# A quarter of the tokens per partition group for two small computations, and a plan that knows GpSimd's port, in a fused attention kernel

## The chip, the cores and the metric

One core of a Trainium2 chip. The metric is the device time of one execution in microseconds, the median of several. A comparison is a ratio: the mean time of one kernel's fast runs over the mean of the other's fast runs of the same rounds, with a 95% interval, so it is not quite the ratio of the medians quoted beside it. In the profile PE is the matrix engine TensorE, PEld its weight loads, ACT is ScalarE, DVE is VectorE, POOL is GpSimd and SP the engine that issues the transfers. PSUM is the memory, in banks, that PE's results go to.

## The reference

Two attentions over the same 2048 tokens (640 features, 32 heads of 20), mixed by a gate. A is full attention, B looks at eight earlier tokens two apart.

```python
g = sigmoid((x * gate_w).sum(-1, keepdims=True))
a = A_ref(x, A_wqkv, A_wo)      # softmax(q k^T * scale) v over all 2048 keys, 32 heads
b = B_ref(x, B_wqkv, B_wo)      # softmax over 8 taps: keys at s, s-2, ..., s-14, masked below 0
return g * a + (1 - g) * b
```

## The kernel before

The kernel is written as generators of tasks. A small scheduler in the same file puts the tasks in order **before** the program exists: it keeps a clock for each engine, with a planned duration for each task and a latency for each engine's results, and decides with it which task comes next on each engine. The chip then runs that fixed order. An engine whose next instruction isn't ready waits, whatever else is ready.

```python
LAT = {"pe": 0.18, "act": 0.06, "dve": 0.08, "pool": 0.1, "sp": 0.1}   # planned latency of results, us
PLAN = {                     # settings of the planner, from the n-th tile of exponentials on
    0: ((0.3, 0.7), 0.26, 2.5, 1.0, 1.0, -1.0, 0.0, 12.0, 7.0, 9.64, ...),
    # ... 56 rows more (cut)
}
# in task(): when may it start, by the plan's clock?
start = self.avail[stream]
for d in t.deps:
    start = max(start, d.end + LAT[d.stream])
```

A's scores are computed by PE in units of 512 keys by queries, 2048 units in all. Two or three units make a tile that ScalarE exponentiates (`ebuf`). Some units, called rides, are left to VectorE: an integer approximation (`uD`) in four shifted copies (`eD`), for which GpSimd scales the values (`vS`). Each such unit costs PE four value products in place of one.

```python
# A: upper bounds of the scores, from |q| and the keys' maxima; 32 partitions, 512 tokens
ins = e.matmul(side[b][0:32, :], KMd[:, ff, :], qabs[qq][:, :], start=(k == 0), stop=(k == len(fl) - 1), ...)
T("dve", dvc(512), lambda e, b=b: e.tensor_scalar(qbnd[0:32, :], side[b][0:32, :], 1.0, STEP * TOP, ...), ...)
# B: gate and denominators; 128 partitions, of which groups of 32 hold the same heads, 256 tokens
mms = [(side[b][:, TOK:2 * TOK], gwrep(c), xT[:, c, t0:t0 + TOK]) for c in range(CN)]
mms = [(side[b][:, 0:TOK], Rep[:, :], eB[:, hh * TOK:(hh + 1) * TOK]) for hh in range(2)]
T("act", actc(TOK), lambda e, b=b: e.activation(tB[:, :], side[b][:, TOK:2 * TOK], ACTF.Tanh, scale=0.5), ...)
t = TB(TOK * 7.5e-3, lambda e, b=b: e.reciprocal(rB[:, :], side[b][:, 0:TOK]), ...)
release(b, t)                # the bank of PSUM may be used again after the reciprocal
# A: the shifted copies of a ride, and the scaled values for them
T("dve", 0.11 + 0.1334 * n, lambda e, k=k, sl=sl: e.tensor_scalar(eD[:, sl % NS, ...], uD[...], SHIFTS[k], ...), ...)
T("pool", 1.0, lambda e: e.tensor_tensor(vS[:, d % 2, :, :], ..., ALU.mult), ...)
```

## Time and profile before

| | before |
|---|---|
| time, median | 850.85 us |
| ScalarE, first to last exponential | 815.8 us |
| of it, its work back to back | 777.8 us |
| of it, lost | 38.0 us |
| PE fillers (sets of four matmuls, run where the plan has nothing else for PE) | 306 |
| rides on VectorE | 328 of 2048 units |

"Work back to back" counts each activation at the distance to its successor when none waits (904 ns for 1024 columns, 1331 ns for 1536, 477 ns for 512, 264 ns for 256, read from the start times); "lost" is the rest. (The prediction put the two at 816.3 and 38.5 us; here the last exponential ends at its start plus its distance.) These rows of the groups by form, besides those that the prediction shows, are needed later. After the bar come busy time in us and the mean of one in ns, after the second bar the engine's idle time before it.

```profile
L792 DVE TENSOR_SCALAR eD<-uD 128x2048 int16<-128x2048 int16 x246 | 174.1, 734 | 3.0 <-PE obank L1545 2.3
L784 POOL TENSOR_TENSOR vS<-vA,vw 128x252 bf16<-128x252 bf16 x82 | 62.9, 769 | 259.7 <-PE obank L1545 259.7
L864 DVE TENSOR_TENSOR stage<-qkvB 128x1280 bf16<-128x1280 bf16 x64 | 53.7, 866 | 0.1
```

The waits (who for whom, us in total, times, longest):

```profile
PEld score L1477 <- ACT ebuf L1500: 105.9, 268, 1.3
PE score L1477 <- ACT ebuf L1500: 6.8, 17, 1.0
PEld score L1477 <- DVE uD L1490: 24.2, 55, 1.1
```

The reader should see that PE's matmuls hardly wait for ScalarE (6.8 us), and not conclude that PE is short of time. Its weight loads wait 105.9 us for ScalarE, mostly while PE is busy with something else (all its idle time is 848.7 - 821.5 = 27.2 us), and 306 fillers of 0.216 us are another 66 us in which the plan had nothing for it.

### The profile page before, as it was taken

The numbers are of one execution on the slowest core, as the hardware profiler recorded it, in microseconds if no ns is written. First come the engines' busy times: TensorE is split into PE (matmuls) and PEld (weight loads), VectorE is DVE, ScalarE is ACT, GpSimd is POOL, SyncE is SP. The second block draws the span as 40 slices with busy tenths as digits, with TensorE's granted clock in tenths as the row PEclk, the third lists the DMA queues.
The fourth block names the chain that finished last, engine by engine and source line by source line (L and its number), as shares of the span: only waits on it lengthen the run. The fifth ranks groups of instructions, "written<-read, shape, count | busy, mean of one in ns | idle before, by whom it ended". The sixth has DMA issues, their size and how long they took to land.

```text
span 848.7 us, 30119 instructions
## 1 busy us (share of the span) xinstructions
PE 821.5 (97%) x12957; PEld 299.7 (35%) x12957; DVE 716.4 (84%) x1212; ACT 809.6 (95%) x770; POOL 142.0 (17%) x181
## 2 busy tenths in 40 slices
PE   8999999999999999999999999999999999999997
PEld 4432232334333343334334243333332333333233
DVE  7566887889899797989888898989998897999973
ACT  4999999999999999999999999999999999999994
POOL 5031014501122110111100111111011111012110
PEclk9999999999999999999999999999999999999999
DMA  9011212001010010011001011010010001001000
GB/s 314 23 40 42 48 31 73 15 13 33 26 27 22 25 42 20 21 25 27 16 16 37 6 20 44 20 31 11 19 32 20 7 20 41 15 7 40 17 6 33
DMA packets 40889, 28.13 MB, mean 33 GB/s; under 512 B 23732, under 2 KB 39556, under 8 KB 40756
## 3 DMA queue, kind: packets, MB, share of 16 engines
q1 hardware_dynamic: 40756, 26.20, 11.8%
q8 instruction: 103, 1.69, 0.8%
q14 instruction: 30, 0.25, 0.1%
HBM read 11.94 MB, written 2.62 MB: 17 GB/s over the span
## 4 chain that ended last, share of the span: by engine, by line
PE 73%; ACT 14%; DVE 8%; issue 5%; SPq 0%; DMA 0%; DVEq 0%; ACTq 0%
PE score L1477 22%; PE obank L1545 18%; PE side L554 16%; ACT ebuf L1500 13%; PE score L554 8%; PE obank L1566 4%; DVE eD L792 2%; PE score L1566 2%; DVE uD L1490 1%; PE side L878 1%; DVE stage L864 1%; PE score L1193 1%; PE obank L457 1%; DVE oN L767 1%; PE score L680 0%
## 5 line engine op out<-in xcount | busy, mean ns | idle before, releaser
L1500 ACT ACTIVATE ebuf<-score 128x1024 bf16<-128x1024 f32 (+1 forms) x738 | 796.5, 1187 | 17.6 <-PE score L1477 14.7
L1477 PE MATMUL score<-qT,kT 32*128 32x512 bf16 x2048 | 295.0, 384 | 9.9 <-ACT ebuf L1500 6.8
L1490 DVE TENSOR_SCALAR uD<-score 128x512 int16<-128x512 f32 x328 | 220.9, 684 | 45.7 <-PE score L1477 42.0
L792 DVE TENSOR_SCALAR eD<-uD 128x2048 int16<-128x2048 int16 x246 | 174.1, 734 | 3.0 <-PE obank L1545 2.3
L1477 PEld LDWEIGHTS score<-qT,kT 32*128 32x128 bf16 x2048 | 72.9, 91 | 263.9 <-ACT ebuf L1500 105.9
L1545 PE MATMUL obank<-ebuf,vA 128*21 128x512 bf16 x1720 | 160.1, 385 | 4.6 <-DVE eD L792 3.5
L784 POOL TENSOR_TENSOR vS<-vA,vw 128x252 bf16<-128x252 bf16 x82 | 62.9, 769 | 259.7 <-PE obank L1545 259.7
L554 PE MATMUL side<-xT,kvw 128*32 128x256 bf16 (+1 forms) x2470 | 101.7, 281 | 0.7 <-DVE qkvB L848 0.6
L1545 PE MATMUL obank<-eD,vS 128*21 128x512 bf16 x984 | 86.0, 379 | 0.0
L760 POOL TENSOR_TENSOR rcp<-rcp,gA 128x16 f32<-128x16 f32 x31 | 12.3, 395 | 386.6 <-DVE rcp L758 367.2
L554 PEld LDWEIGHTS side<-xT,kvw 128*32 128x32 bf16 x2470 | 58.4, 96 | 34.9 <-issue 16.7
L1545 PEld LDWEIGHTS obank<-ebuf,vA 128*21 128x21 bf16 x1720 | 38.6, 89 | 89.3 <-issue 72.9
L1566 PE MATMUL obank<-xT,zero 128*32 128x512 bf16 x688 | 58.5, 383 | 0.0
L864 DVE TENSOR_TENSOR stage<-qkvB 128x1280 bf16<-128x1280 bf16 x64 | 53.7, 866 | 0.1
L941 DVE TENSOR_TENSOR stage<-qkvB,repB 128x1280 bf16<-128x1280 bf16 x64 | 52.6, 848 | 1.0 <-DMA repB<-eB 1.0
L554 PE MATMUL side<-stage,ident 128*32 128x512 bf16 (+1 forms) x736 | 46.7, 345 | 1.0 <-DVE oB L956 0.5
L848 DVE CAST qkvB<-side 128x512 bf16<-128x512 f32 (+1 forms) x70 | 40.5, 587 | 6.4 <-PE side L554 6.4
L765 POOL TENSOR_TENSOR oN<-oTt,rcp 128x512 bf16<-128x512 f32 x31 | 34.8, 1123 | 2.4
L1566 PE MATMUL score<-xT,ident 128*32 128x512 bf16 x380 | 33.7, 381 | 0.0
L1545 PE MATMUL obank<-uD,vA 128*21 128x512 bf16 x328 | 31.9, 379 | 0.0
L754 DVE STREAM_TRANSPOSE oTt<-obank 128x512 f32<-128x512 f32 x32 | 22.8, 712 | 8.9 <-PE obank L1545 8.6
L1545 PEld LDWEIGHTS obank<-eD,vS 128*21 128x21 bf16 x984 | 24.5, 91 | 15.5 <-issue 1.8
(175 smaller groups left out, 622.8 us busy)
## 6 DMA issues: line engine op xcount, KB each, us to landing
repB<-eB SPq DMA_DIRECT2D x128, 32.0 KB
WqP<-in_A_wqkv_dram SPq DMA_DIRECT2D x16, 160.0 KB
stage<-in_B_wqkv_dram SPq DMA_DIRECT2D x1, 2400.0 KB
oTd<-oN SPq DMA_DIRECT2D x108, 20.0 KB
qT<-dst SPq DMA_DIRECT2D x104, 20.0 KB
out_dram<-outsb SPq DMA_DIRECT2D x12, 160.0 KB
kvw<-in_A_wqkv_dram SPq DMA_DIRECT2D x2, 800.0 KB
oTd<-in_A_x_dram SPq DMA_DIRECT2D x2, 640.0 KB
```

What stands on the lines that cost most here:

```text
L554: ins = e.matmul(o[j:k, :], l[:, j:k], r, start=(first and i == 0), stop=(last and i == n - 1), skip_group_check=True)
L765: T(en, c2, lambda e: e.tensor_tensor(oo, ii, ib, ALU.mult), reads=["rcp", "oTt"], writes=["oN0"])
L784: T("pool", 1.0, lambda e: e.tensor_tensor(vS[:, d % 2, :, :], _ap(vA, (kb * NQ + q) * 4 * DV, [[0, K - 1], [1, 4 * DV]]), _ap(vw, 0, [[1, ...
L792: T("dve", 0.11 + 0.1334 * n, lambda e, k=k, sl=sl: e.tensor_scalar(eD[:, sl % NS, 0:512 * n].bitcast(I16), uD[d % 2][:, 0:512 * n].bitcas ...
L848: t = TB(dvc(n * TOK), lambda e, o=o, i=i: e.tensor_copy(o, i), reads=[("side", b)], writes=[key])
L864: TB(dvc(CN * TOK, 2), lambda e, w=w, ks=ks: e.tensor_tensor(prodB(w), qB[:, :, :], ks, ALU.mult), reads=["qB", "kB"], writes=[("prod", w) ...
L941: TB(dvc(CN * TOK, 2), lambda e, w=w, vs=vs, rr=rr: e.tensor_tensor(prodB(w), vs, rr, ALU.mult), reads=["vB", ("repB", w4 % 2)], writes=[( ...
L1477: ins = e.matmul(o, kT[32 * j:32 * j + 32, q, kb * P:(kb + 1) * P], qT[g % NQT][32 * j:32 * j + 32, :], start=True, stop=True)
L1490: t = T("dve", 0.69, lambda e: e.tensor_scalar(uD[d % 2][:, 512 * i:512 * (i + 1)].bitcast(I16), side[x], UOFF, 0.0, op0=ALU.add, op1=ALU. ...
L1500: exps[s] = T("act", actc(512 * n), lambda e: e.activation(ebuf[s % NE][:, 0:512 * n], score[s % 2][:, 0:512 * n], ACTF.Exp, scale=LN2 / S ...
L1545: ins = e.matmul(obank[32 * j:32 * j + DV, :], v, src, start=(kb == 0), stop=(last and k >= len(lst) - 4), skip_group_check=True)
L1566: ins = e.matmul(o[32 * j:32 * j + 32, :], w[:, 32 * j:32 * j + 32] if best else w[:, :], xT[:, 0, 0:512], start=bool(best), stop=bool(bes ...
```

## The change

Its intent: bounds, gate and denominators use only 32 partitions' worth of different rows. A quarter of the tokens goes to each group of 32 partitions, so that PE streams and VectorE evicts a quarter of the columns, and transfers bring the result into the layout wanted. The plan gets longer latencies, a model of the port that VectorE and GpSimd share, and a new table.

```diff
-LAT = {"pe": 0.18, "act": 0.06, "dve": 0.08, "pool": 0.1, "sp": 0.1}
+LAT = {"pe": 0.22, "act": 0.18, "dve": 0.13, "pool": 0.15, "sp": 0.1}
+        port = stream == "pool" and not dma or port
+        if port:
+            for a, b in sorted(self.port["dve" if stream == "pool" else "pool"][-8:]):
+                if a < start + dur and start < b:
+                    start = b
+            self.port[stream].append((start, start + dur))
 PLAN = {   # the whole table is new (cut), as are some eighteen constants of the planner and GpSimd's planned durations
-            ins = e.matmul(side[b][0:32, :], KMd[:, ff, :], qabs[qq][:, :], ...)
+            for j in range(4):
+                ins = e.matmul(side[b][32 * j:32 * j + 32, 0:P], KMd[:, ff, :], qabs[qq][:, j * P:(j + 1) * P], ...)
-    ... e.tensor_scalar(qbnd[0:32, :], side[b][0:32, :], 1.0, STEP * TOP, ...)
+    ... e.tensor_scalar(qbnd[:, :], side[b][:, 0:P], 1.0, STEP * TOP, ...)        # and four transfers for one
-    t = TB(TOK * 7.5e-3, lambda e, b=b: e.reciprocal(rB[:, :], side[b][:, 0:TOK]), ...)
+    t = TB(TQ * 7.5e-3, lambda e, b=b: e.reciprocal(rQ[:, :], side[b][:, 0:TQ]), ...)     # TQ = TOK // 4
+    T("sp", 2.0 + 0.5 * 4, lambda e: [e.dma_start(rB[0:32, j * TQ:(j + 1) * TQ], rQ[32 * j:32 * j + 32, :]) ...
+    spread = lambda: T("sp", 2.0 + 0.5 * 3, lambda e: [e.dma_start(rB[32 * i:32 * i + 32, :], rB[0:32, :]) ...
 # gate, denominators and tanh likewise; port=True on the VectorE tasks that use the port (cut)
```

## The prediction

> **What bounds the kernel now.** I read the page's busy line first, then its slices, the chain of waits, the groups by form, and the waits of ScalarE.
>
> ```profile
> span 848.7 us, 30119 instructions
> PE 821.5 (97%) x12957; PEld 299.7 (35%) x12957; DVE 716.4 (84%) x1212; ACT 809.6 (95%) x770; POOL 142.0 (17%) x181
> ...
> ACT  4999999999999999999999999999999999999994
> ...
> PEclk9999999999999999999999999999999999999999
> ...
> PE 73%; ACT 14%; DVE 8%; issue 5%; SPq 0%; DMA 0%; DVEq 0%; ACTq 0%
> ```
>
> Three engines are nearly full and the clock is never reduced. Two things soften PE's 97%. First, PE runs filler matmuls where the plan has nothing else (the L1566 rows below). Second, matmul records overlap: a set of four 512-column matmuls records 379 ns but its successor starts 216 ns later (starts read from the trace). ScalarE has no filler: its work is the exponentials. That the chain still names PE for 73% says in which form ScalarE is made late: the score matmuls reach it late because PE, which works strictly in the order that the plan wrote, was still at something else.
>
> ```profile
> L1500 ACT ACTIVATE ebuf<-score 128x1024 bf16<-128x1024 f32 x492 | 476.5, 1043 | 10.1 <-PE score L1477 8.2 <-ACT ebuf L1500 0.3
> L1500 ACT ACTIVATE ebuf<-score 128x1536 bf16<-128x1536 f32 x245 | 344.3, 1479 | 7.2 <-PE score L1477 6.3 <-ACT ebuf L1500 0.3
> L1566 PE MATMUL obank<-xT,zero 128*32 128x512 bf16 x688 | 58.5, 383 | 0.0
> L1566 PE MATMUL score<-xT,ident 128*32 128x512 bf16 x380 | 33.7, 381 | 0.0
> L1566 PE MATMUL side<-xT,ident 128*32 128x512 bf16 x156 | 12.0, 382 | 0.0
> L680 PE MATMUL score<-qabs,KMd 128*32 128x512 bf16 x28 | 8.6, 382 | 0.1
> L922 DVE RECIPROCAL rB<-side 128x256 f32<-128x256 f32 x7 | 12.3, 1754 | 5.9 <-ACT tB L919 5.9
> L687 DVE TENSOR_SCALAR qbnd<-score 32x512 bf16<-32x512 f32 x15 | 10.1, 672 | 2.4 <-PE score L680 2.4
> L924 DVE SCALAR_TENSOR_TENSOR rB<-tB,rB 128x256 f32<-128x256 f32 x8 | 3.4, 425 | 0.3
> L919 ACT ACTIVATE tB<-side 128x256 f32<-128x256 f32 x7 | 3.1, 436 | 0.0
> ...
> ACT ebuf L1500 <- PE score L1477: 14.7, 36, 2.1
> ```
>
> The reader should see that the idle time of ScalarE in these rows (17.3 us) understates what it loses, as successive activations overlap in the records. From their start times, back to back, a 1024-column exponential follows its predecessor after 904 ns, a 1536-column one after 1331 ns, a 512-column one after 477 ns. So 492 x 0.904 + 245 x 1.331 + 0.5 = 771.4 us of exponentials; with eight 512-column activations for B (3.8), eight 256-column tanh at 0.264 (2.1) and the gates (0.5) it is 777.8 us. The first exponential starts at 19.9 and the last ends at about 836.2, 816.3 us. ScalarE thus loses **38.5 us** between them; 20 us of start and 12.5 us of tail lie outside.
>
> **What the Trainium skill says.** (1) "Perfetto Trace Analysis", Identifying the Most-Contended Engine: occupancy is a fair measure for Scalar and Vector, matmul busy time is not one for TensorE. The trace agrees: PE is "97%" busy with 306 filler sets in it. (2) "SBUF — State Buffer", Who interferes with whom: a DVE instruction in a two-port mode, or with two SBUF inputs beside a GpSimd read, contends with GpSimd, and the second to issue blocks fully. The trace agrees for eD (L792): median 683 ns in the 198 that no GpSimd instruction overlaps, 869 ns in the 48 that one does, up to 1827 ns. All of it above the clear median is 12.5 us. The B products (L864, L941) exceed their clear median by 5.3 us together. (3) "TensorEngine Tiling (Array Packing)", Key Properties: changing the tiling mode drains TensorE. Here the start of the score rows after a column-tiled set is about 0.1 us later than the set's columns explain, and the same on the way back. Its section Instruction Overhead puts a floor of some 60 cycles under a matmul; here sets of four 128-column matmuls follow each other in 56 ns, of 256 in 109 ns, and no 64-column set is in this trace.
>
> **The change part by part**, with counts from the two programs' instruction orders.
>
> *Score bounds.* 36 matmuls of 512 columns on one column group, 216 ns apart, become 36 sets of four with 128 columns, 56 ns: 7.8 to 2.0, **-5.8 us on PE**. The 20 evictions (L687) go from 512 to 128 columns on all partitions; a cast of 128 columns (L1079) takes 277 ns, so 20 x (0.672 - 0.277) = **-7.9 us on DVE**. The 42 transfers become four times as many; one holds its queue 556 ns (median), so +126 x 0.556 = 70 us on the SP queue.
>
> *B's denominators and gate.* Gate: 40 sets from 256 to 64 columns, at most 109 to 56 ns, -2.1 us; denominators: 16 sets, -0.8 us. **-2.9 us on PE.** Tanh from 264 to, with the slope 0.833 ns per column of the exponentials, some 104 ns: **-1.3 us on ScalarE**. Reciprocal: the line through 243 ns for 16 columns (L758) and 1754 ns for 256 gives about 545 ns for 64, 8 x 1.21 = -9.7 us; the gate product (L924) loses about 0.2 us each, -1.6 us. **-11.3 us on DVE.** Spreading adds 8 x 7 transfers, 31 us of SP queue. They run beside the eight products of a B unit (8 x 0.85 us), which come before the first reader of rB, so I expect them hidden.
>
> *The new plan.* It hands over 316 score units (512 keys by queries) to DVE instead of 328, and packs the other 1732 into 724 exponentials (438 of 1024, 285 of 1536, one of 512) instead of 738. ScalarE: 438 x 0.904 + 285 x 1.331 + 0.5 = 775.8, **+4.4 us**. DVE: -12 x 0.684 - 9 x 0.734 = **-14.8 us**. PE: nine sets of value matmuls fewer, -1.9; 14 score sets with two mode changes, 14 x (0.216 + 0.2) = -5.8: **-7.7 us**. Fillers fall from 306 sets to 235: 15 us, but they are no work.
>
> *Port and latencies in the plan.* They cost nothing to run. They move DVE instructions that need the shared port away from GpSimd's, and let the plan wait for results when they come (its latency after ScalarE goes from 0.06 to 0.18 us). At most the 17.8 us of stretched DVE instructions go; I expect about half.
>
> Sums: PE -16.4 us without fillers, DVE -34.0 us and perhaps -9 more, ScalarE +3.1 us. What of it is on the path? PE leads 73% of the chain, so 0.73 x 16.4 = 12.0 us if its savings lie evenly. DVE leads 8%, 68 us, and loses 34.0/716 = 4.7% of its work: 3.2 us. ScalarE's +3.1 us count in full. Net -12.1 us. I take a little off, since the saved time only counts where a score set was late, and a plan can put another side task into it: **-10.5 us, so about 840.5 us.** Put otherwise, ScalarE's lost time would fall from 38.5 to some 25 us.
>
> **The rivals.** *(a) ScalarE is the floor, and the change frees the wrong engines.* DVE and PE get lighter, but ScalarE gets 3.1 us more; if its lost time is due to mode changes and the handshake of two score buffers rather than to PE's load, nothing is gained: 850 to 854 us. For it: the late chain (570 to 760 us) is mostly ScalarE, and 122 of its delays are of 60 to 300 ns, handshake size. Against: 23.5 us of the lost time come from 34 delays over 300 ns, which a handshake does not make. *(b) The plan now fits the chip and nearly all long delays go.* Then lost time falls to 15 us or less: 816.3 + 3.1 - 23.5 = 796 us from first to last exponential, about 830 us. For it: DVE is wrongly planned now (eD planned at 0.644 us, measured 0.734), the plan was searched anew, and PE work per exponential falls by 2%. Against: some of the delays are at the start, where projections fill PE, and at the drain, which the change leaves alone. *(c) The transfers bite.* About 182 more issues, bursts of 8 to 12 at 0.556 us, can hold the tap transfers that the B products wait for, or a query tile. Now DVE waits only 1.0 us for the taps and PE hardly for queries. I give this 2 to 6 us on top, 843 to 847 us.
>
> **Range and chances.** 840.5 us, between (b)'s 830 and (a)'s 850 with (c) inside. Both ends are mechanisms that I can defend, and the new plan is a different order everywhere, whose luck I cannot read: 830 to 849 holds it 8 in 10. Two per cent faster is 833.8 us, which needs the lost time cut from 38.5 to about 18 us: 0.18. Slower by two per cent is 867.9 us: 0.02. Within: 0.80.
>
> **What would show it.** Right: L922's successor near 545 ns, the bound evictions near 277 ns, tanh near 104 ns apart; eD's mean falling from 734 towards 700 ns; DVE busy near 680 us; exponentials over 300 ns late well below 34; ScalarE's lost time near 25 us with the same 20 us before the first exponential. Wrong: ScalarE's lost time unchanged while DVE and PE are lighter (rival a); under 18 us (rival b); DVE rows with idle time on a DMA of rB, repB or qT above 3 us (rival c). The step I trust least is the share of PE's savings on the path.

## The result, and the profile after

The changed kernel takes **844.7 us** (844.51 to 845.46) against 850.9 us; the ratio is 0.9928 with an interval from 0.9911 to 0.9945: faster by 0.7%, within 2%. The page after, busy time and chain of waits:

```profile
span 843.0 us, 29847 instructions
PE 791.8 (94%) x12745; PEld 294.8 (35%) x12745; DVE 683.2 (81%) x1191; ACT 808.4 (96%) x756; POOL 137.9 (16%) x178
...
PE 44%; ACT 38%; issue 11%; DVE 5%; SPq 1%; DMA 0%; DVEq 0%; ACTq 0%
```

The groups by form that answer to those of before:

```profile
L1529 ACT ACTIVATE ebuf<-score 128x1024 bf16<-128x1024 f32 x438 | 424.6, 1056 | 8.6 <-PE score L1506 6.2 <-ACT ebuf L1529 0.4 <-PE side L560 0.2
L1529 ACT ACTIVATE ebuf<-score 128x1536 bf16<-128x1536 f32 x285 | 398.1, 1492 | 5.7 <-PE score L1506 5.3
L799 DVE TENSOR_SCALAR eD<-uD 128x2048 int16<-128x2048 int16 x237 | 168.8, 738 | 11.0 <-PE obank L1574 10.3
L871 DVE TENSOR_TENSOR stage<-qkvB 128x1280 bf16<-128x1280 bf16 x64 | 50.6, 822 | 0.1
L694 DVE TENSOR_SCALAR qbnd<-score 128x128 bf16<-128x128 f32 x18 | 5.1, 285 | 3.8 <-PE score L687 2.3 <-DMA qT<-qbnd 1.4
L945 DVE RECIPROCAL rQ<-side 128x64 f32<-128x64 f32 x8 | 4.4, 553 | 4.2 <-ACT tB L942 3.5 <-PE obank L1574 0.6
```

And the waits:

```profile
ACT ebuf L1529 <- PE score L1506: 11.5, 23, 2.1
PEld score L1506 <- ACT ebuf L1529: 116.3, 276, 1.2
PE score L1506 <- ACT ebuf L1529: 27.2, 69, 1.0
PEld score L1506 <- DVE uD L1519: 34.3, 76, 0.9
```

The roles have begun to turn: PE now waits 27.2 us for ScalarE, and ScalarE leads 38% of the chain instead of 14%. Part of that is only another name for the same time: 71 fillers fewer (235 for 306) are 15 us that counted as PE's work before. The same accounting of ScalarE as before gives where the 5.7 us of the span came from:

| us | before | after | difference |
|---|---|---|---|
| until the first exponential | 19.9 | 20.0 | +0.1 |
| ScalarE's work back to back | 777.8 | 780.9 | +3.1 |
| lost between first and last exponential | 38.0 | 30.5 | -7.5 |
| after the last exponential | 13.0 | 11.7 | -1.3 |
| span | 848.7 | 843.0 | -5.7 |

Of the lost time, delays over 300 ns fell from 34 (17.0 us) to 28 (14.4 us), those of 60 to 300 ns from 122 (16.5 us) to 87 (12.4 us). So 7.5 us of lost time were won and 3.1 us of work were added. The question of the experiments is what won them: the lighter parts, or the new order, and through which engine.

### The profile page after: what moved, and what is told of

Read it like the earlier page. It is cut to its first block, busy times and chain, and to the rows that moved or that the text cites. A ratio compares the mean times of both kernels' runs of the same rounds, so it can differ in the third digit from the quotient of the medians.

```text
span 843.0 us, 29847 instructions
## 1 busy us (share of the span) xinstructions
PE 791.8 (94%) x12745; PEld 294.8 (35%) x12745; DVE 683.2 (81%) x1191; ACT 808.4 (96%) x756; POOL 137.9 (16%) x178
## 3 DMA queue, kind: packets, MB, share of 16 engines
q1 hardware_dynamic: 44884, 27.25, 12.4%
## 4 chain that ended last, share of the span: by engine, by line
PE 44%; ACT 38%; issue 11%; DVE 5%; SPq 1%; DMA 0%; DVEq 0%; ACTq 0%
ACT ebuf L1529 37%; PE score L1506 13%; PE side L560 12%; PE obank L1574 10%; PE score L560 4%; PE obank L1595 2%; DVE uD L1519 1%; DVE eD L799 1%; SPq L707 1%; PE score L1222 1%; PE obank L463 1%; PE score L1595 1%; PE side L885 0%; DVE qkvB L855 0%; ACT eB L914 0%
## 5 line engine op out<-in xcount | busy, mean ns | idle before, releaser
L1529 ACT ACTIVATE ebuf<-score 128x1024 bf16<-128x1024 f32 (+1 forms) x724 | 796.9, 1227 | 14.4 <-PE score L1506 11.5
L1506 PE MATMUL score<-qT,kT 32*128 32x512 bf16 x2048 | 287.0, 384 | 34.7 <-ACT ebuf L1529 27.2
L1519 DVE TENSOR_SCALAR uD<-score 128x512 int16<-128x512 f32 x316 | 211.1, 682 | 42.1 <-PE score L1506 39.8
L799 DVE TENSOR_SCALAR eD<-uD 128x2048 int16<-128x2048 int16 x237 | 168.8, 738 | 11.0 <-PE obank L1574 10.3
L560 PE MATMUL side<-xT,kvw 128*32 128x256 bf16 (+1 forms) x2600 | 108.9, 282 | 2.4 <-DVE dst L664 0.8
L1574 PE MATMUL obank<-eD,vS 128*21 128x512 bf16 x948 | 82.0, 379 | 0.0
L560 PEld LDWEIGHTS side<-xT,kvw 128*32 128x32 bf16 x2600 | 61.2, 96 | 38.2 <-issue 18.8
L767 POOL TENSOR_TENSOR rcp<-rcp,gA 128x16 f32<-128x16 f32 x31 | 10.5, 340 | 350.9 <-DVE rcp L765 350.9
L871 DVE TENSOR_TENSOR stage<-qkvB 128x1280 bf16<-128x1280 bf16 x64 | 50.6, 822 | 0.1
L1595 PE MATMUL obank<-xT,zero 128*32 128x512 bf16 x532 | 43.9, 383 | 0.0
L774 DVE STREAM_TRANSPOSE oN<-oN 128x512 bf16<-128x512 bf16 x32 | 22.5, 704 | 11.3 <-POOL oN L772 11.0
L560 PE MATMUL side<-woA_d,oTd 128*32 128x128 bf16 (+1 forms) x600 | 30.7, 295 | 0.0
```

Of the source, the lines that this page charges most:

```text
L560: ins = e.matmul(o[j:k, :], l[:, j:k], r, start=(first and i == 0), stop=(last and i == n - 1), skip_group_check=True)
L871: TB(dvc(CN * TOK, 2), lambda e, w=w, ks=ks: e.tensor_tensor(prodB(w), qB[:, :, :], ks, ALU.mult), reads=["qB", "kB"], writes=[("prod", w) ...
L1506: ins = e.matmul(o, kT[32 * j:32 * j + 32, q, kb * P:(kb + 1) * P], qT[g % NQT][32 * j:32 * j + 32, :], start=True, stop=True)
L1519: t = T("dve", 0.69, lambda e: e.tensor_scalar(uD[d % 2][:, 512 * i:512 * (i + 1)].bitcast(I16), side[x], UOFF, 0.0, op0=ALU.add, op1=ALU. ...
L1529: exps[s] = T("act", actc(512 * n), lambda e: e.activation(ebuf[s % NE][:, 0:512 * n], score[s % 2][:, 0:512 * n], ACTF.Exp, scale=LN2 / S ...
L1574: ins = e.matmul(obank[32 * j:32 * j + DV, :], v, src, start=(kb == 0), stop=(last and k >= len(lst) - 4), skip_group_check=True)
```

## The experiments

Two kinds. In the first, an instruction order is kept, and an engine's time is changed inside the instructions or by one more beside them, so that little but that time differs. In the second, the planner plans anew.

### The changed kernel's order with time put back

`a_pe_back` streams columns that nobody reads, in the places where the change removed them:

```diff
                     for k, (ff, qq) in enumerate(fl):
+                        e.matmul(side[b][0:32, P:512], KMd[:, ff, :], qabs[qq][:, P:512], start=(k == 0), stop=False, ...)
                         for j in range(4):
                             ins = e.matmul(side[b][32 * j:32 * j + 32, 0:P], KMd[:, ff, :], ...)
 # likewise 192 more columns beside each set of the gate and of the denominators
```

> The changed kernel in its own instruction order, with the PE time of the removed matmuls put back: 384 more columns beside each of the 36 bound passes (36 x 160 ns = 5.8 us) and 192 more columns beside each of the 56 gate and denominator sets (56 x 80 ns = 4.5 us), in all 10.2 us of PE, written to columns nobody reads. Theory 1, the step of the prediction: PE's time is on the path for 73% of the span, so the kernel gets about 7.5 us slower, near 852 us. Theory 2: at this order PE waits for ScalarE anyway and the extra columns vanish in those waits: less than 2.5 us slower, 845 to 847 us, and the gain of the change came from the new order.

Measured: 847.3 us, ratio to before 0.9958 (0.9946 to 0.9970), result correct. Against the changed kernel's 0.9928 that is 0.30%, **2.6 us for 10.2 us of PE time**. Theory 1, the share of 73%, falls; theory 2 is near, though 2.6 is just over its 2.5. The pages show where most of the time came from: PE's idle time, the span less its busy time, falls from 51.2 to 45.3 us.

`a_dve_back` does the same with VectorE:

```diff
-    e.tensor_scalar(qbnd[:, :], side[b][:, 0:P], ...)
+    (e.tensor_scalar(scr[:, 0:256]..., sap(b, 0, [[0, 2], [1, P]]), ...), e.tensor_scalar(qbnd[:, :], side[b][:, 0:P], ...))[1]
-    e.reciprocal(rQ[:, :], side[b][:, 0:TQ])
+    (e.reciprocal(scr[:, 0:192]..., sap(b, 0, [[0, 3], [1, TQ]])), e.reciprocal(rQ[:, :], side[b][:, 0:TQ]))[1]
```

> The changed kernel in its own order, with VectorE's removed time put back: 20 scalings of 256 columns and 8 reciprocals of 192 columns into a scratch tile, about 20 x 0.4 + 8 x 1.35 = 19 us of VectorE. Theory 1: the chain's 8% share of VectorE gives 0.05 x 0.08 x 843, about 2 us slower, near 847 us. Theory 3: VectorE is what lets the plan keep its promises (tight waits of PE for VectorE's banks), and a third or more of the 19 us shows: 6 us or more, 851 us or above.

Measured: 855.3 us, ratio 1.0050 (1.0036 to 1.0065), correct: 1.2%, **10.6 us for the 19 us of VectorE time** of the expectation (by the distances in the trace, 20 x 0.33 + 8 x 1.27 us, it is nearer 17). The six runs fall into two groups: 853.1 to 854.2 us at a granted clock of 0.998 to 0.999, and 856.4 to 856.9 at 0.994. The changed kernel had 0.998 to 1.000, so at a like clock the cost is about 9 us. Theory 1's 8% falls as well, to the other side; theory 3 holds. The waits of this run show through what:

```profile
ACT ebuf L1533 <- PE score L1510: 20.2, 34, 2.1
PE side L561 <- DVE rQ L949: 7.7, 8, 1.6
```

In the changed kernel PE's `side` sets wait 0.4 us for `rQ`, once. Here it waits at each of the eight reciprocals, 7.7 us together, and ScalarE's wait for scores rises by 8.7 us, from 11.5 to 20.2. The bank of PSUM is released after the reciprocal, and the plan had put PE's next use of that bank right there. The score matmuls stand behind it in PE's order.

`a_both_back` puts back both, so that the new order carries about the work of the old parts.

> The changed kernel's order with both the PE time (10.2 us) and the VectorE time (19 us) put back, so that the engines have nearly the work of before in the new order. If the two costs add, 844.7 + 2.6 + 10.6 = 858 us. Theory O: the new order was made for the lighter parts and is worse than the old order at the old load: above 855 us. Rival: the new order is better by itself, as it was made with truer latencies: below the 850.8 us of before.

Measured: 857.6 us, ratio 1.0082 (1.0068 to 1.0096), correct. The two costs add (2.6 + 10.6 against 12.9; at a like clock 2.5 + 9 against 12), and the new order with the old load is **slower than before** by 6.9 us. Theory O holds, the rival falls: the new order isn't better by itself at the old load.

### The old order with time taken away

`b_pe_off` and `b_dve_off` take the same times from the kernel before without moving an instruction. Their results are wrong; in `b_pe_off` the later instructions keep their sizes by reading the same columns repeatedly.

```diff
-    ins = e.matmul(side[b][0:32, :], KMd[:, ff, :], qabs[qq][:, :], ...)
+    ins = e.matmul(side[b][0:32, 0:P], KMd[:, ff, :], qabs[qq][:, 0:P], ...)           # b_pe_off
-    e.reciprocal(rB[:, :], side[b][:, 0:TOK])
+    e.reciprocal(rB[:, :], side[b][:, 0:TOK]) if u == 0 else e.reciprocal(rB[:, 0:64], side[b][:, 0:64])   # b_dve_off
 # likewise gate and denominators (b_pe_off), bound evictions and gate product (b_dve_off)
```

> The kernel before in its own order, with the same PE time taken away (bound passes stream 128 columns, gate and denominator sets 64; the results are wrong on purpose, the later instructions keep their sizes by reading the same columns four times): 10.2 us of PE less. Theory 1: 7.5 us faster, near 843.5 us. Theory 2: under 2.5 us faster, 848 to 851 us.

> The kernel before in its own order, with VectorE's time taken away: all but the first bound eviction at 128 columns, all but the first reciprocal and gate product at 64 columns (results wrong on purpose): 19 x 0.39 + 7 x 1.4 = 17 us of VectorE less. Theory 1: about 2 us faster, near 849 us. Theory 3: 5 us or more faster, 846 us or below.

> The old order with both times taken away (results wrong on purpose). If the two add, 850.8 - 1.1 - 1.1 = 848.6 us. Theory O: an order fixed in advance cannot turn freed time into speed, so it stays at 847 us or above although its engines now have less work than the changed kernel's (328 rides, 737 exponentials apart). Rival: the two freed engines were each other's cover, and only both together show: 845 us or less.

Measured: `b_pe_off` 849.5 us, ratio 0.9989 (0.9977 to 1.0001); `b_dve_off` 849.7 us, 0.9988 (0.9975 to 1.0001); `b_both_off`, which has both edits, 848.8 us, 0.9973 (0.9960 to 0.9985). Taking 10 us of PE and 17 us of VectorE away wins **2 us**; each alone is not clear of no gain at all. For PE theory 1 falls and theory 2 holds: PE's idle time rises from 27.2 to 33.3 us (on the pages), so more than half of what was taken away only became idle. For VectorE theory 3 falls, but theory 1's 2 us lie within the interval. The rival of `b_both_off`, 845 us or less, falls too. With the runs above they make a table of two by two (`b_both_off` leaves the shorter tanh and the added transfers out):

| us | heavy parts | light parts |
|---|---|---|
| order of before | 850.9 (the kernel before) | 848.8 |
| order of the changed kernel | 857.6 | 844.7 (the changed kernel) |

Neither the parts alone (-2) nor the order alone (+7) makes the gain of 6 us; it takes both. That an order made for light parts suffers under heavy ones is no surprise, and the table doesn't say what an order made as carefully for the heavy parts would reach. The section on planning anew asks that.

### The shared port

`a_vs_small` and `b_vs_small` keep each kernel's order and cut GpSimd's scaled values to four columns (wrong).

```diff
-    vS[:, d % 2, :, :], _ap(vA, ..., [[0, K - 1], [1, 4 * DV]]), _ap(vw, 0, [[1, K - 1], [0, 4 * DV]]), ALU.mult)
+    ... if d < 2 else e.tensor_tensor(vS[:, d % 2, 0, 0:4], _ap(vA, ..., [[1, 4]]), _ap(vw, 0, [[0, 4]]), ALU.mult)
```

> The kernel before in its own order with the same cut of vS: 8.7 us of stretched VectorE time go. Theory P1: under 1 us faster. Theory P3: this plan does not know of the port, so the stretched instructions come as surprises and their absence is worth more than in the changed kernel: 3 us or more, 848 us or below. Theory O: as with the other time taken away from this order, about 1 us.

> The changed kernel's order with GpSimd's scaled values (vS) cut from 252 columns to 4 after the first two (results wrong on purpose): GpSimd holds the shared port for less than 0.2 us instead of 0.61 us, 79 times, so the 9.9 us by which vS stretches VectorE's eD and product instructions go. Theory P1, the prediction's share: 8% of it shows, under 1 us. Theory P2: VectorE's unplanned time shows for about half, as when it was put back (10.6 of 19 us): 4 to 5 us faster, near 840 us. Theory P3: the plan has these waits in it, so their absence only becomes idle time: under 1 us.

`b_vs_small` took 847.6 us, ratio 0.9961 (0.9949 to 0.9974): 3.1 us by the medians for some 9 us of stretched VectorE time. `a_vs_small` took 843.6 us, 0.9914 (0.9901 to 0.9928), 1.1 us below the changed kernel, and the two intervals overlap. Groups of `b_vs_small`, then of `a_vs_small`:

```profile
L793 DVE TENSOR_SCALAR eD<-uD 128x2048 int16<-128x2048 int16 x246 | 166.8, 704 | 3.1 <-PE obank L1546 2.5
L785 POOL TENSOR_TENSOR vS<-vA,vw 128x4 bf16<-128x4 bf16 x80 | 28.3, 356 | 277.6 <-PE obank L1546 277.6
```

```profile
L800 DVE TENSOR_SCALAR eD<-uD 128x2048 int16<-128x2048 int16 x237 | 161.3, 707 | 11.5 <-PE obank L1575 10.7
L792 POOL TENSOR_TENSOR vS<-vA,vw 128x4 bf16<-128x4 bf16 x77 | 27.6, 358 | 311.9 <-PE obank L1575 291.5 <-PE score L687 11.8 <-PE score L1507 4.6
```

In both the mean eD falls by about 30 ns (from 734 and 738), so the same stretch was removed, and only the order without the port in its plan gains clearly by it. GpSimd's own work got shorter too, but no wait for `vS` stands in the list of waits of before, so the gain is hardly an earlier `vS`. Theory P3 fits the old order, and the changed kernel nearly (1.1 us for under 1); P1 says the same there, but falls on the old order, as does theory O; P2 falls. So an order fixed in advance can turn freed time into speed: here 9 us on VectorE gave 3 us, where the 17 us of `b_dve_off` gave 1. Which time it is decides.

The port model did not make eD's collisions go: what eD takes above its clear median while GpSimd runs is 12.8 us before and 13.7 after. Those of the B products did go, from 5.6 to 2.0 us (the mean of L864 and L871 above, 866 to 822 ns). That the model's worth is to have counted the rest is the likely reading of the two runs, but no run takes the port alone out of a plan.

### Planning anew

A table of 54 tuned rows is made for one set of tasks and falls apart when a task changes, so a planner with one part undone can't be compared as it stands. Three kernels were therefore tuned alike: the table replaced by its first row, then a random search of about 15,000 trials that lowers the clock that the plan itself keeps. A fourth kept the table and got other durations.

```diff
 # tune_new_parts: the changed kernel with a table made by the search
 # tune_old_parts: the same, with bounds, gate and denominators as before
 # tune_old_model: tune_new_parts with
-LAT = {"pe": 0.22, "act": 0.18, "dve": 0.13, "pool": 0.15, "sp": 0.1}
+LAT = {"pe": 0.18, "act": 0.06, "dve": 0.08, "pool": 0.1, "sp": 0.1}
-        port = stream == "pool" and not dma or port
+        port = False
 # calibrated: the changed kernel, its table searched on, with
-    actc = lambda n: 0.08 + n * 0.8334e-3
+    actc = lambda n: 0.051 + n * 0.8334e-3        # latency act 0.18 -> 0.21
-    dvc = lambda n, mode=1: 0.10 + n * 1.0417e-3 / mode
+    dvc = lambda n, mode=1: 0.067 + n * 1.0417e-3 / mode        # latency dve 0.13 -> 0.165
```

> The changed kernel with its table of plan settings thrown away and made anew from one row by a plain random search (14170 trials) that lowers the clock which the plan itself keeps. That clock ends at 858.6 us; the changed kernel's own ends at 846.1 and took 844.7 us on the chip. If the new plan's clock holds its promise within 3 us, this kernel takes 855 to 860 us. It is the base for the next two, tuned in the same way and as long.

> The same new plan and the same search (14359 trials from the same one row), with the old parts: bounds on 32 partitions, reciprocal and gate at 256 columns. Its clock ends at 864.0 us. Theory L (the lighter parts pay once the plan is made for them): 4 to 8 us slower than tune_new_parts, near 862 us. Rival M (the gain came from the truer latencies, not from the parts): within 2 us of tune_new_parts.

> The new parts, the same search (16682 trials from the same one row), but with the latencies of before in the plan and no port. Its clock ends at 848.7 us, 10 us earlier than tune_new_parts' clock. Theory M: that clock is too early, as that of before was (its clock 836.0, chip 850.9): 862 us or more, 4 us or more slower than tune_new_parts. Rival: the clock is only another yardstick, and the kernel takes 855 us or less.

> The changed kernel with its plan's durations set to the distances between successive instructions that its trace shows (exponential 0.051 us + 0.8334 ns per column in place of 0.080; VectorE's fixed part 0.067 in place of 0.10, the ride 0.605 in place of 0.69), the latencies raised by the same amounts so that results come no earlier, and the table searched on from its own (14170 trials). Its clock ends at 839.6 us. If that clock is as true as the last one (846.1 for 844.7), 838 to 842 us, faster than both kernels. If the search only used errors of the model, 846 us or more.

| kernel | plan's clock | measured | plan early by | ScalarE's work | ScalarE lost | rides |
|---|---|---|---|---|---|---|
| before | 836.0 | 850.9 | 14.9 | 777.8 | 38.0 | 328 |
| changed | 846.1 | 844.7 | -1.4 | 780.9 | 30.5 | 316 |
| tune_new_parts | 858.6 | 865.6 | 7.0 | 794.2 | 38.2 | 288 |
| tune_old_parts | 864.0 | 868.5 | 4.5 | 798.5 | 35.4 | 280 |
| tune_old_model | 848.7 | 868.4 | 19.7 | 781.9 | 53.5 | 316 |
| calibrated | 839.6 | 858.1 | 18.5 | 781.1 | 43.9 | 316 |

The ratios to before are 1.0175 (1.0162 to 1.0188), 1.0219 (1.0187 to 1.0250), 1.0217 (1.0202 to 1.0232) and 1.0091 (1.0073 to 1.0110). `tune_new_parts` missed its own expectation: its clock was early by 7.0 us, not by less than 3. By the medians the old parts cost 2.9 us, but two of the four runs of `tune_old_parts` had a lower granted clock (870.3 us at 0.992, 874.8 at 0.986), and its verdict is "unclear". The other two took 865.7 and 866.7 us at 0.996 and 0.997, against 865.3 to 866.1 at 0.998 for `tune_new_parts`. So at a like clock the old parts cost about 1 us or less, which fits rival M (within 2 us) and not theory L. The old latencies cost 2.4 to 2.8 us: the 862 us of theory M are passed, its 4 us are not reached, and its rival (855 us) falls. One search of each was run, so differences of 3 us are weak evidence. What is plain is the shape. With the old latencies the plan hands over 28 rides more and gives ScalarE 12 us less work, and ScalarE then loses 15 us more. A good part of that is two waits near the start, 3.1 and 4.4 us (the longest of `tune_new_parts` is 1.2), the second behind a transfer of bounds on which PE stood. That the rest comes of results later than the plan believes is likely, and not shown:

```profile
ACT ebuf L1545 <- PE score L1522: 25.2, 42, 4.3
PE score L1522 <- DMA qT<-qbnd: 3.9, 1, 3.9
```

(waits of `tune_old_model`), against these of `tune_new_parts`:

```profile
ACT ebuf L1543 <- PE score L1520: 16.1, 31, 2.1
```

`calibrated` failed twice. It took 858.1 us (856.3 to 861.8, at a granted clock of 0.989 to 0.996) where its clock promised 839.6, and its result was wrong (relative error 0.33), which was not intended; why is not settled, and a wrong result could also mean that the search found an order that leaves the planner's own rules. Its time speaks only for this: distances between undisturbed neighbours are not enough to make the plan's clock true. The changed kernel's clock seems close to the chip partly because its errors offset each other. It plans an exponential 29 ns longer than the undisturbed distance (0.933 us for 1024 columns against 0.904), 724 times, 21 us; the lost 30.5 us are about the same size. No run with a right result was faster than the changed kernel.

## Why the prediction was right or wrong

The time was inside the range and on the side of the lesser gain, and "within 2%" was right. The step that was mis-sized is the sum's last, "What of it is on the path? PE leads 73% of the chain, so 0.73 x 16.4 = 12.0 us", with its second half, the 3.2 us for VectorE's 8%. The gain was 6.1 us where 10.5 were forecast, and ScalarE's lost time fell to 30.5 us, not to 25. That the measured time lies inside the range is in part luck: it lies where rival (c) put it, and the transfers are hardly the reason (see the rivals below).

- **ScalarE as the floor, and its added work.** Right: +3.1 us forecast and +3.1 us found, from counts and distances alone. The start was unchanged, as forecast.
- **PE's share.** Wrong. 10.2 us of PE time are worth 0.9 to 1.2 us in the old order and 2.6 us in the new one, 9 to 25% and not 73%; some 6 us of them came out of PE's idle time or went into it. The share of the chain counts how long PE's instructions led it, fillers among them; it doesn't say that what would come after them could come earlier. In a fixed order the next instruction has waits of its own.
- **VectorE's share.** Too small where the time was put back: some 17 to 19 us cost 9 to 10.6 us in the new order, most of it by the waits through eight reciprocals that hold a bank that PE wants next. Taken away in the old order, 17 us are worth 1 us (interval 0 to 2), which doesn't contradict the share (3.2 for 34 us, so 1.6 for 17). One number for the engine can't say both.
- **The parts.** Right in size on VectorE: the reciprocal takes 553 ns (545 forecast), the bound eviction 285 (277), the tanh 104 apart (104), VectorE's busy time is 683 us (near 680). PE saved somewhat more than said: 64-column sets are 29 ns apart, not up to 56.
- **The port.** Wrong in the sign to look for. "eD's mean falling from 734 towards 700 ns" did not happen (738). On eD the plan moved collisions rather than removing them: another task of GpSimd, `oN`, no longer stretches it (4.2 us before), while `vS` (6.1 to 8.0) and the weight copies (2.7 to 5.9) stretch it more. Only the B products' stretch fell. (Counted again, the stretch before is 12.8 and 5.6 us, where the prediction has 12.5 and 5.3; 15.7 of 18.4 us are left, not half.) Undoing those by `vS` gains 3.1 us in the old order and 1.1 in the new.
- **"DVE is wrongly planned now (eD planned at 0.644 us, measured 0.734)."** This compared unlike things. 734 ns is the recorded length; undisturbed eD instructions follow each other after about 600 ns. VectorE's time was planned a little too long and its results too early, and the change corrected the latter.
- **Lost time over 300 ns.** The prediction put 23.5 us on 34 delays. Between first and last exponential it is 17.0 us on that number of delays; a wait of ScalarE at the very end (7.3 us, at L1045) probably makes the difference. Rival (b) rested on this sum. 28 delays remain, less of a fall than forecast.
- **The rivals.** (a), ScalarE gets more and wins nothing: half right, it gives back 3.1 of the 7.5 us. (b), nearly all delays go: no. (c), transfers: VectorE waits 1.4 us for bound transfers and 0.2 us for the taps, below the 3 us that had been named as their sign.

What stays open is how the 7.5 us divide between lighter parts, latencies, port and table, and whether the old parts with a table made as well would be as fast. The retuned kernels point to the truer latencies for some of the lost time and leave the parts at about 1 us or less, but these differences are small beside what the table itself is worth: the same tasks take 844.7 us with the changed kernel's table and 865.6 us with one from the short search.

## What to carry to other kernels

In a kernel with an order fixed in advance, don't price a saving by an engine's share of the chain: keep the order, put the time back (or take it away) inside the instructions, and measure. Without a new plan, 27 us freed on two engines gave 2 us and 9 us freed at other places of VectorE gave 3; added time showed at once where it held a buffer that the next engine was waiting for. Three planners' clocks here were early by 15 to 20 us, and a search that lowers such a clock did not lower the time on the chip, so compare the clock with the chip before tuning by it. And compare runs at a like granted clock: a difference of 2.9 us here mostly went with the clock.

## What the Trainium skill lacked or had wrong

- "SBUF — State Buffer", Who interferes with whom: its rule fits (eD 683 ns clear, up to 1827 ns beside GpSimd), but it gives no notion of what blocking is worth to a kernel. Here about 9 us of stretched VectorE instructions were worth 3.1 us in one order and 1.1 us in another.
- "Perfetto Trace Analysis", Optimization Strategy: it says to find what blocks the engine that one optimizes and to make that start sooner or complete faster, and not how much of such a saving arrives. In an order fixed in advance it was little: 27 us taken from two engines gave 2 us. I found no page that treats this.
- The same page's occupancy as a fair measure for Scalar: recorded lengths of neighbours overlap (1043 ns recorded, 904 ns apart), so ScalarE's idle time of 17.3 us in its two rows hid 38.0 us of lost time. The page notes elsewhere that recorded lengths overlap, but doesn't carry it into this measure.
- "TensorEngine Tiling (Array Packing)", Instruction Overhead: four matmuls on four column groups share one period, 29 ns at 64 columns, 56 at 128, 109 at 256. The page has no figure for a set of four; "TensorE: Matmul & The Clock Gate" has a span for one pack of tiles, not the distance between packs of four column groups.
